# First weight columns ahead of the second chunk of x, three more dummy matmuls, and new stage settings in a gated attention and mixer kernel

## The chip, the cores and the metric

The kernel runs on one core of a Trainium2 chip. The time is device microseconds of one execution, as the median of several; the kernel before took 788.51 us (787.51 to 789.9) in its first three runs; each batch of runs had a chip of its own, and before ran beside it.

Names: PE is TensorE, ACT ScalarE, DVE VectorE, POOL GpSimd, SP the engine that issues most DMA. In the profile, L909 is line 909 of the kernel.

## The reference

```python
def reference(A_x, A_wqkv, A_wo, B_x, B_w1, B_w2, B_w3, B_w4, gate_w):
    def _A_ref(x, wqkv, wo):                     # 32 heads of 16, S = 2048, D = 512
        ...
        scores = jnp.einsum("bhqd,bhkd->bhqk", q, k) * (Dh ** -0.5)
        p = _softmax(scores, axis=-1)
        o = jnp.einsum("bhqk,bhkd->bhqd", p, v)
        return (...)(o, 0, 2, 1, 3).reshape(B, S, D) @ wo
    def _B_ref(x, w1, w2, w3, w4):
        h = _gelu(_layernorm(x, axis=-1) @ w1)
        ...                                      # shifts of h along S by quarters of D
        x1 = x + hs                              # hs = shifted h @ w2
        return x1 + _gelu(_layernorm(x1, axis=-1) @ w3) @ w4
    g = _sigmoid((x * gate_w).sum(-1, keepdims=True))
    return g * a + (1 - g) * b                   # a = _A_ref(x), b = _B_ref(x)
```

There are 32 x 2048 x 2048 exponentials, cut into 2048 score tiles of 128 x 512 with four heads side by side; they are the bulk of the work of ACT and DVE.

## The kernel before

The order of the instructions of every engine is fixed when the kernel is built, by a small model of the engines in Python. The model is steered by some twenty settings, and STAGES overrides them for each stretch of 32 score tiles. Other lines only say what must come before what.

The head: transfers that start before the model does, each with an assumed latency in ns, and dummy matmuls that keep PE busy until x lands.

```python
    xa, xb = (start(e, 3000.0, lambda q, a=a: q.dma_start(out=x_sb[:, a:a + 2, :], in_=x_src(0, a, a + 2)))
              for e, a in (("SP", 0), ("ACT", 2)))
    j_x0 = [xa, xb]
    dl_w["k0"] = start("ACT", 2300.0, col(W("k"), D, D + 128))
    dl_w["q0"] = start("ACT", 2300.0, col(wq, 0, 128))
    j_x1 = [start("SP", 4900.0, lambda q: q.dma_start(out=x_sb[:, 4:8, :], in_=x_src(1, 0, 4)))]
    ...
    def warm_pe():
        for _ in range(8):
            nc.tensor.matmul(sim_ring[RING - 1][:, 0:384], lhsT=zero[:, 0:P], rhs=zero[:], start=True, stop=True)
```

The exponentials on DVE: a pair of tiles is made with a bit trick (L935), and three shifted copies of it follow, on DVE (L971) or on POOL (L974). Which engine makes which copy is up to the settings (GP2, GP3, URG). The model knows that POOL's instructions and these copies exclude each other (`port`).

```python
        for k in range(1, 4):
            def sh(k=k):
                d = [b.slot for b in bufs]
                if alone or k == 1 or k == 2 and not both:
                    nc.vector.tensor_scalar(out=d[k][:, 0:w], in0=d[0][:, 0:w], scalar1=float(SHIFT * k), scalar2=None,
                                            op0=ALU.add)
                else:
                    nc.gpsimd.tensor_scalar(out=d[k][:, 0:w], in0=d[0 if both else 2][:, 0:w], scalar1=1.0,
                                            scalar2=float(SHIFT * (k if both else 1)), op0=ALU.mult, op1=ALU.add)
            ...
                j = dve(0.26 * w + 72.0, pr["jobs"], sh, prio=K.S_PRIO, acq=[bufs[k]], frees=[bufs[0]], port=True)
```

The layer norm (L682): DVE writes a normalised row tile into one of two buffers `xn`, from which a DMA writes it to DRAM, to be read back transposed. The third tile has to wait until the first write is through.

```python
        for t in range(4 * c, 4 * c + 4):
            xb = Buf("xn", 1)
            g = dve(323, [m], lambda t=t, xb=xb: nc.vector.tensor_scalar(
                out=xb.slot[:], in0=x_sb[:, t, :], scalar1=rs[which][:, t:t + 1], scalar2=nm[which][:, t:t + 1],
                op0=ALU.mult, op1=ALU.add), prio=0.35, acq=[xb], port=True)
            ds.append(dma(2200.0, [g], lambda t=t, xb=xb: nc.sync.dma_start(
                out=xn_dram[which, t * P:(t + 1) * P, :], in_=xb.slot[:]), frees=[xb]))
```

The softmax here doesn't subtract the row's maximum and nothing guards it: scores larger than these inputs give would overflow.

## Time and profile before

| before | us |
|---|---|
| profiled span | 787.5 |
| head, up to ACT's first exp | 14.50 |
| body, first to last exp of ACT | 763.20 |
| tail | 9.80 |
| busy in the body: PE, ACT, DVE, POOL | 750.8, 738.0, 737.2, 335.3 |

The cut at ACT's first and last exp parts what can be reasoned about by hand (the head: a chain of transfers and a few instructions) from what cannot (the body: three engines busy for 97 to 98% of it, which hand work to each other). The prediction shows the lines.

### The profile page before, as it was taken

How to read it: one execution, taken by the hardware profiler on the slowest of the kernel's cores; microseconds unless marked ns; L12 is line 12 of the kernel's file. 1: busy time of each engine (PE TensorE's matmuls, PEld its weight loads, DVE VectorE, ACT ScalarE, POOL GpSimd, SP SyncE). 2: the span in 40 equal slices, each digit the busy share in tenths (PEclk: the TensorE clock that was granted, in tenths of full speed). 3: DMA queues.
4: the chain of work that ended last, by engine and by line, in shares of the span. 5: the costliest groups of instructions: out<-in, count | busy, mean ns of one | idle time of the engine just before them, and what ended most of it. 6: DMA issues, size and time to landing. Idle time of an engine off the chain costs nothing.

```text
span 787.5 us, 23893 instructions
## 1 busy us (share of the span) xinstructions
PE 766.7 (97%) x9672; PEld 227.1 (29%) x9672; DVE 744.9 (95%) x1587; ACT 743.3 (94%) x764; POOL 339.2 (43%) x331
## 2 busy tenths in 40 slices
PE   7999999999999999999999999999999999999997
PEld 3433322222222222223222223222223222223222
DVE  4999999999999999999998999899999999999996
ACT  4899999999999999999999999999999999999995
POOL 2234544344546443444244443344434345445352
PEclk9999999999999999999999999999999999999999
DMA  8302113423000320062101001001100000000101
GB/s 204 123 16 46 37 46 80 91 45 113 20 6 20 83 59 20 25 152 62 29 11 32 23 20 46 19 18 36 43 18 20 15 22 26 26 20 20 17 6 44
DMA packets 67093, 34.60 MB, mean 44 GB/s; under 512 B 46748, under 2 KB 62380, under 8 KB 66984
## 3 DMA queue, kind: packets, MB, share of 16 engines
q1 hardware_dynamic: 65512, 32.43, 16.7%
q8 instruction: 75, 1.23, 0.7%
q10 hardware_dynamic: 1472, 0.66, 0.3%
q14 instruction: 34, 0.28, 0.1%
HBM read 17.40 MB, written 6.81 MB: 31 GB/s over the span
## 4 chain that ended last, share of the span: by engine, by line
PE 57%; DVE 23%; ACT 12%; issue 3%; DMA 3%; SPq 1%; POOL 0%; ACTq 0%; POOLq 0%; DVEq 0%
PE acc L1005 20%; PE ring L519 18%; PE psA L829 18%; DVE PD L935 9%; ACT PA L909 9%; DVE PD L971 7%; DMA xn_dram<-xn 1%; PE ring L829 1%; DVE st L662 1%; DMA wq<-in_A_wqkv_dram 1%; DVE V L605 1%; ACT hT L722 1%; ACT hT L753 1%; ACT hB L753 1%; DVE hB L752 1%
## 5 line engine op out<-in xcount | busy, mean ns | idle before, releaser
L909 ACT ACTIVATE PA<-psA 128x1024 bf16<-128x1024 f32 x739 | 693.4, 1040 | 25.0 <-PE acc L1005 8.7
L974 POOL TENSOR_SCALAR PD<-PD 128x1024 uint16<-128x1024 uint16 x269 | 283.8, 1058 | 418.2 <-DVE PD L971 263.0
L935 DVE TENSOR_SCALAR PD<-ring 128x512 uint16<-128x512 f32 x570 | 374.4, 682 | 17.8 <-PE ring L829 15.0
L1005 PE MATMUL acc<-PD,V 128*17 128x512 bf16 x2280 | 302.3, 381 | 2.6 <-DVE accsb L1021 1.4
L829 PE MATMUL psA<-q,kT 32*128 32x512 bf16 x1478 | 284.7, 384 | 3.4 <-ACT PA L909 3.1
L1005 PE MATMUL acc<-PA,V 128*17 128x512 bf16 x1478 | 269.7, 381 | 0.2 <-DVE accsb L1021 0.2
L971 DVE TENSOR_SCALAR PD<-PD 128x1024 uint16<-128x1024 uint16 x586 | 241.4, 453 | 3.5 <-PE acc L1005 1.7
L829 PE MATMUL ring<-q,kT 32*128 32x512 bf16 x570 | 195.4, 384 | 2.8 <-DVE PD L935 2.5
L829 PEld LDWEIGHTS <-kT 32*128 32x128 bf16 x2048 | 73.9, 91 | 306.2 <-issue 305.1
L1005 PEld LDWEIGHTS <-V 128*17 128x17 bf16 x3758 | 74.4, 88 | 141.3 <-issue 119.7
L519 PE MATMUL ring<-xnT,w 128*32 128x512 bf16 x1152 | 91.4, 383 | 1.9 <-DVE qf L588 1.5
L519 PE MATMUL ring<-w,hT 128*32 128x512 bf16 x704 | 58.2, 383 | 0.2 <-DVE PD L935 0.2
L519 PEld LDWEIGHTS <-w 128*32 128x32 bf16 x1920 | 43.5, 95 | 49.7 <-issue 37.8
L1038 POOL TENSOR_TENSOR oT<-accsb,bcs 128x512 bf16<-128x512 f32 x31 | 40.3, 1301 | 10.9 <-DMA bcs<-rr 7.5
L519 PE MATMUL ring<-w,w 128*32 128x256 bf16 (+1 forms) x768 | 41.0, 316 | 0.8 <-DVE PD L935 0.8
L519 PE MATMUL ring<-w,hB 128*32 128x512 bf16 x448 | 35.1, 383 | 0.0
L519 PE MATMUL ring<-w,wq 128*32 128x512 bf16 x256 | 21.2, 398 | 2.8 <-DMA wq<-in_A_wqkv_dram 2.3
L1021 DVE COPY accsb<-acc 128x512 f32<-128x512 f32 x31 | 21.1, 682 | 1.5 <-POOL oT L1038 0.9
L662 DVE BATCH_NORM_STATS2 st<-x_sb 128x6 f32<-128x512 bf16 x32 | 21.6, 682 | 0.0
L519 PEld LDWEIGHTS <-hT 128*32 128x32 bf16 x704 | 14.7, 95 | 19.3 <-issue 14.7
L752 DVE CAST hB<-ring 128x512 bf16<-128x512 f32 x28 | 18.9, 680 | 0.8 <-PE ring L519 0.7
L752 DVE CAST hT<-ring 128x512 bf16<-128x512 f32 x28 | 19.0, 684 | 0.2 <-PE ring L519 0.2
(93 smaller groups left out, 285.2 us busy)
## 6 DMA issues: line engine op xcount, KB each, us to landing
bcs<-rr SPq DMA_DIRECT2D x124, 64.0 KB
xn_dram<-xn SPq DMA_DIRECT2D x32, 128.0 KB
w<-in_B_w_dram SPq DMA_DIRECT2D x5, 512.0 KB
oD<-oT SPq DMA_DIRECT2D x124, 16.0 KB
w<-in_B_w_dram SPq DMA_DIRECT2D x4, 448.0 KB
out_dram<-ot SPq DMA_DIRECT2D x14, 128.0 KB
x_sb<-in_A_x_dram SPq DMA_DIRECT2D x3, 512.0 KB
w<-in_A_wqkv_dram SPq DMA_DIRECT2D x2, 256.0 KB
```

The costliest lines, as they stand in the source:

```text
L519: units.append([Op("col", j, lambda j=j, lf=lf, rf=rf, n0=n0, n1=n1, st=st, sp=sp: nc.tensor.matmul(get()[32 * j:32 * j + 32, n0:n1], lhsT ...
L662: a = dve(600, deps, lambda: nc.vector.bn_stats(out=sb.slot[:], in_=x_sb[:, t, :]), prio=6, at=at, acq=[sb])
L752: pre.append(evac(g, PSUM_NS, lambda ps, m=m: nc.vector.tensor_copy(out=h2()[:, m, :], in_=ps[:])))
L753: ge = act(93 + 427 * FT + 2600, pre, lambda: nc.scalar.activation(out=h2(), in_=h2(), func=ACT.Gelu_apprx_tanh), prio=0)
L829: o = Op("row", i, lambda: nc.tensor.matmul(dst(), lhsT=kT[G][32 * i:32 * i + 32, kt * P:(kt + 1) * P], rhs=qbuf[G, c].slot[32 * i:32 * i ...
L909: job = act(hold, ops, lambda: nc.scalar.activation(out=pb.slot[:, 0:n], in_=buf.slot[:, 0:n], func=ACT.Exp, scale=0.25), acq=[pb], frees= ...
L935: nc.vector.tensor_scalar(out=pr["buf"].slot[:, h * 512:(h + 1) * 512], in0=buf.slot[:], scalar1=BITS_MUL, scalar2=BITS_ADD, op0=ALU.mult, ...
L971: nc.vector.tensor_scalar(out=d[k][:, 0:w], in0=d[0][:, 0:w], scalar1=float(SHIFT * k), scalar2=None, op0=ALU.add)
L974: nc.gpsimd.tensor_scalar(out=d[k][:, 0:w], in0=d[0 if both else 2][:, 0:w], scalar1=1.0, scalar2=float(SHIFT * (k if both else 1)), op0=A ...
L1005: o = Op("col", i, lambda: nc.tensor.matmul(acc[32 * i:32 * i + DH + 1, :], lhsT=lhs(), rhs=rhs(), start=st, stop=True, tile_position=(0, ...
L1021: e = dve(PSUM_NS, round_ops[r], lambda: nc.vector.tensor_copy(out=ab.slot[:], in_=acc[:]), acq=[ab], prio=0)
L1038: n = gp(1250, d3, lambda: nc.gpsimd.tensor_tensor(out=ob.slot[:], in0=ab.slot[:], in1=bb.slot[:], op=ALU.mult), acq=[ob], frees=[ab, bb], ...
```

## The change

Its intent: the first query columns, which the first projection waits for, no longer share the DMA engines with the second chunk of x; more dummies keep PE's clock awake until the projections; and the settings are chosen anew for the changed head.

```diff
-    STAGES = {0: {'DUE_SH': -20, 'AHEAD': 7, 'GP2': 0.35}, 2: {'S_PRIO': 0.324}, ... (cut)
+    STAGES = {0: {'S_PRIO': 0.539, 'DUE_SH': -40}, 1: {'PA_LOW': 1}, 2: {'DVE_WAIT': 2, 'PV_FULL': 0.877}, ... (cut)
@@
-    dl_w["k0"] = start("ACT", 2300.0, col(W("k"), D, D + 128))
-    dl_w["q0"] = start("ACT", 2300.0, col(wq, 0, 128))
+    dl_w["q0"] = start("SP", 2600.0, col(wq, 0, 128))
+    dl_w["k0"] = start("ACT", 2900.0, col(W("k"), D, D + 128))
     j_x1 = [start("SP", 4900.0, lambda q: q.dma_start(out=x_sb[:, 4:8, :], in_=x_src(1, 0, 4)))]
@@
     def warm_pe():
-        for _ in range(8):
+        for _ in range(11):
```

More of the change, by code (lines that the diff above doesn't have):

```diff
@@ L309 @@
     SEG = 32
-    STAGES = {0: {'DUE_SH': -20, 'AHEAD': 7, 'GP2': 0.35}, 2: {'S_PRIO': 0.324}, 3: {'SL': (125, 60), 'AT_SH': 120}, 4: {'ROT': 2, 'DVE_STOP': 7, 'DUE_SH': -8, 'GP2': 0.35}, 5: {'ROT': 2}, 6: {'AHEAD': 8, 'GP2': 0.1, 'P1_PRIO': 0.54}, 7: {'DVE_STOP': 9, 'P1_PRIO': 0.53}, 8: {'DUE_SH': 40, 'URG_L': 19, 'AT_SH': 60}, 9: {'GP2': 0.35, 'DVE_WAIT': 2, 'EARLY': 20, 'PV_IDLE': 0.245}, 10: {'GP3': 0.6}, 11: {'IDLE_NS': 706, 'GP2': 0.35}, 13: {'PV_IDLE': 0.414, 'SL': (5, 60), 'IDLE_NS': 296}, 14: {'GP3': 0.9, 'AT_SH': 120}, 15: {'ROT': 3, 'P1_PRIO': 0.554, 'PV_FULL': 0.948}, 16: {'GP2': 0.1, 'EARLY': 141}, 17: {'AT_SH': 10}, 18: {'GP2': 0.35, 'MAXU': 4}, 19: {'GP2': 0.35, 'P1_PRIO': 0.522, 'SL': (165, 180), 'DVE_WAIT': 2}, 20: {'EARLY': 145, 'S_PRIO': 0.286, 'GP2': 0.1}, 21: {'EARLY': 145, 'S_PRIO': 0.286, 'GP2': 0.1}, 22: {'AHEAD': 11, 'AT_SH': 10, 'EARLY': 51}, 23: {'AT_SH': 10}, 24: {'ROT': 2, 'URG': 3, 'GP3': 0.8}, 25: {'PD_LOW': 2}, 26: {'SL': (125, 60), 'DUE_SH': 40, 'S_PRIO': 0.248, 'AHEAD2': 8}, 27: {'ROT': 1, 'URG_L': 15, 'AHEAD': 12}, 28: {'PRESS': 21, 'P1_PRIO': 0.544, 'S_PRIO': 0.282}, 29: {'PV_IDLE': 0.462, 'DVE_STOP': 4}, 30: {'GP3': 0.9, 'PRESS': 21}, 31: {'GP3': 0.6}, 32: {'DVE_WAIT': 6, 'ROT': 2, 'DUE_SH': 40}, 34: {'DUE_SH': 40, 'DVE_ALONE': 2, 'GP3': 0.6}, 35: {'IDLE_NS': 471, 'DUE_SH': 20, 'DVE_STOP': 5, 'MAXU': 3}, 36: {'GP2': 0.1, 'PRESS': 14}, 37: {'DVE_ALONE': 2, 'DVE_STOP': 3, 'EARLY': 31, 'PA_LOW': 3}, 38: {'PD_LOW': 3, 'EARLY': 55, 'PA_LOW': 2, 'URG': 7}, 39: {'S_PRIO': 0.456, 'AHEAD2': 7, 'EARLY': 155, 'ROT': 1}, 40: {'PA_LOW': 3, 'DVE_ALONE': 2, 'GP3': 0.8}, 41: {'URG': 8, 'URG_L': 19}, 42: {'URG_L': 19, 'PRESS': 39, 'ROT': 1}, 43: {'GP3': 0.8}, 44: {'PD_LOW': 1}, 45: {'DVE_WAIT': 2, 'AHEAD2': 10}, 46: {'GP3': 0.6}, 47: {'DUE_SH': -40, 'EARLY': 79, 'MAXU': 9, 'PA_LOW': 2}, 48: {'DVE_ALONE': 300, 'ROT': 1}, 49: {'AT_SH': 120, 'P1_PRIO': 0.475}, 50: {'IDLE_NS': 896, 'PD_LOW': 2, 'ROT': 2, 'PA_LOW': 1}, 51: {'PD_LOW': 1, 'URG': 6, 'DVE_ALONE': 150, 'IDLE_NS': 830}, 52: {'PRESS': 53, 'EARLY': 6, 'IDLE_NS': 668, 'PV_FULL': 0.848}, 53: {'AHEAD': 12, 'AT_SH': 10, 'PA_LOW': 2, 'ROT': 3}, 54: {'DVE_STOP_L': 6, 'GP3': 0.9}, 55: {'DUE_SH': -40, 'PV_IDLE': 0.253, 'DVE_STOP_L': 10, 'PA_LOW': 2}, 56: {'SL': (25, 60), 'PA_LOW': 2}, 57: {'ROT': 1, 'SL': (85, 60)}, 58: {'GP3': 0.8, 'PD_LOW': 3, 'URG_L': 19}, 59: {'GP2': 0.1}, 60: {'DUE_SH': -20, 'GP3': 0.6, 'P1_PRIO': 0.409}, 61: {'GP2': 0.2}, 62: {'DVE_STOP_L': 10, 'MAXU': 6, 'PA_LOW': 2, 'AHEAD2': 11}, 63: {'DVE_STOP_L': 6, 'MAXU': 6, 'ROT': 1}, 64: {'DVE_STOP_L': 6, 'MAXU': 6, 'SL': (165, 180)}}
@@ new lines @@
+    STAGES = {0: {'S_PRIO': 0.539, 'DUE_SH': -40}, 1: {'PA_LOW': 1}, 2: {'DVE_WAIT': 2, 'PV_FULL': 0.877}, 4: {'GP2': 0.35, 'GP3': 0.8}, 7: {'PV_FULL': 0.918, 'S_PRIO': 0.302}, 8: {'AHEAD2': 6, 'PA_LOW': 0, 'PD_LOW': 1, 'AHEAD': 12}, 9: {'ROT': 3}, 10: {'PD_LOW': 3, 'AHEAD': 12}, 11: {'DVE_STOP_L': 11, 'GP2': 0.35}, 12: {'PRESS': 38, 'AT_SH': 120, 'ROT': 2, 'SL': (5, 20)}, 13: {'DVE_STOP_L': 11, 'PD_LOW': 3}, 14: {'PV_IDLE': 0.491, 'ROT': 3}, 15: {'DVE_WAIT': 5, 'ROT': 2}, 16: {'EARLY': 112, 'DVE_ALONE': 500, 'PD_LOW': 0}, 17: {'ROT': 1, 'DVE_ALONE': 300}, 18: {'AHEAD': 11, 'S_PRIO': 0.52}, 19: {'AT_SH': 60}, 21: {'MAXU': 7, 'PA_LOW': 0, 'IDLE_NS': 490, 'PRESS': 15}, 22: {'AHEAD': 10, 'GP2': 0.2, 'DVE_ALONE': 150, 'MAXU': 11}, 23: {'AT_SH': 10, 'PA_LOW': 0}, 24: {'AT_SH': 10, 'IDLE_NS': 358}, 25: {'PV_FULL': 0.882, 'SL': (125, 140)}, 26: {'PV_IDLE': 0.486, 'DVE_STOP_L': 6, 'DVE_WAIT': 5, 'PV_FULL': 0.856}, 27: {'AT_SH': 120}, 28: {'DVE_WAIT': 2, 'PRESS': 23, 'SL': (5, 20), 'PV_FULL': 0.918}, 29: {'DVE_WAIT': 5, 'DVE_STOP': 4, 'GP2': 0.35, 'DVE_STOP_L': 6}, 31: {'EARLY': 150, 'PD_LOW': 3, 'DUE_SH': 8}, 32: {'DVE_STOP_L': 7, 'S_PRIO': 0.449, 'SL': (25, 60), 'GP2': 0.1}, 33: {'AT_SH': 30, 'GP3': 0.9, 'AHEAD2': 7}, 34: {'PA_LOW': 2, 'P1_PRIO': 0.295}, 35: {'DVE_STOP_L': 9, 'ROT': 2}, 37: {'ROT': 3}, 38: {'P1_PRIO': 0.235, 'PRESS': 14}, 39: {'DVE_ALONE': 300, 'GP2': 0.2}, 40: {'GP3': 0.6, 'PV_FULL': 0.994}, 41: {'PRESS': 15}, 42: {'SL': (205, 60), 'PD_LOW': 2}, 43: {'GP3': 0.9, 'GP2': 0.35}, 44: {'P1_PRIO': 0.218, 'DVE_STOP_L': 9, 'GP2': 0.35, 'IDLE_NS': 726}, 45: {'DVE_STOP_L': 7, 'S_PRIO': 0.577}, 46: {'DVE_WAIT': 6, 'ROT': 2}, 47: {'PV_FULL': 0.857, 'AT_SH': 60, 'DVE_STOP': 8}, 48: {'DVE_ALONE': 0, 'AHEAD': 10, 'DUE_SH': 80, 'ROT': 1}, 49: {'IDLE_NS': 285, 'GP3': 0.8, 'DUE_SH': -8, 'PD_LOW': 1}, 50: {'PD_LOW': 3}, 51: {'GP3': 0.6, 'ROT': 3}, 52: {'PV_FULL': 1, 'DVE_STOP_L': 11}, 53: {'S_PRIO': 0.29, 'DVE_STOP': 5}, 54: {'GP3': 0.8, 'PA_LOW': 2, 'IDLE_NS': 527}, 55: {'DVE_STOP_L': 6, 'P1_PRIO': 0.319, 'S_PRIO': 0.229}, 56: {'GP2': 0.35, 'ROT': 1}, 57: {'AHEAD2': 6, 'PA_LOW': 2, 'IDLE_NS': 417, 'S_PRIO': 0.31}, 58: {'GP2': 0.35}, 59: {'GP2': 0.35}, 60: {'P1_PRIO': 0.366, 'MAXU': 5, 'EARLY': 16, 'GP2': 0.2}, 61: {'AHEAD2': 11, 'PV_FULL': 0.984, 'DVE_STOP': 9}, 62: {'PRESS': 45, 'PD_LOW': 2, 'IDLE_NS': 491, 'P1_PRIO': 0.424}, 63: {'PRESS': 45, 'PD_LOW': 2, 'IDLE_NS': 491, 'P1_PRIO': 0.424}}
```

## The prediction

> **What bounds the kernel now.** I read the busy shares first, then the costliest groups, then busy time by stretch (head, body, tail), then the chain and the TensorE timeline of the first 16 us. The shares say that three engines are loaded alike:
>
> ```profile
> PE 766.7 (97%) x9672; PEld 227.1 (29%) x9672; DVE 744.9 (95%) x1587; ACT 743.3 (94%) x764; POOL 339.2 (43%) x331
> PE   7999999999999999999999999999999999999997
> DVE  4999999999999999999998999899999999999996
> ACT  4899999999999999999999999999999999999995
> ```
>
> Only the first slice (20 us) of DVE and ACT is half empty; the rest is 9 nearly everywhere. The groups show why: softmax's exponentials are shared between ACT (a true exp of two score tiles at a time) and DVE (a bit trick on one tile at a time, whose result is copied with shifts by DVE or POOL and fed four times to PE).
>
> ```profile
> L909 ACT ACTIVATE PA<-psA 128x1024 bf16<-128x1024 f32 x739 | 693.4, 1040 | 25.0 <-PE acc L1005 8.7
> L974 POOL TENSOR_SCALAR PD<-PD 128x1024 uint16<-128x1024 uint16 x269 | 283.8, 1058 | 418.2 <-DVE PD L971 263.0
> L935 DVE TENSOR_SCALAR PD<-ring 128x512 uint16<-128x512 f32 x570 | 374.4, 682 | 17.8 <-PE ring L829 15.0
> ...
> L971 DVE TENSOR_SCALAR PD<-PD 128x1024 uint16<-128x1024 uint16 x586 | 241.4, 453 | 3.5 <-PE acc L1005 1.7
> ```
>
> I cut the span where ACT's first exp starts (14.50 us) and where its last ends (777.7 us). Columns: stretch, its length, then busy us (and instructions) of PE, PEld, DVE, ACT, POOL, then clock, DMA share and GB/s.
>
> ```profile
> 0.00:14.50 14.50, 10.30 (x77) 4.98 (x77) 3.65 (x10) 4.10 (x7) 3.87 (x14) 1.00 0.98 226
> 14.50:777.70 763.20, 750.79 (x9524) 219.08 (x9525) 737.20 (x1570) 737.95 (x756) 335.31 (x317) 1.00 0.16 40
> 777.70:787.50 9.80, 5.62 (x81) 3.00 (x70) 4.02 (x8) 1.29 (x3) 0.00 (x0) 1.00 0.16 54
> ```
>
> In the body ACT idles 763.20 - 737.95 = 25.3 us, DVE 26.0 us. PE idles 12.4 us, but its busy time holds 14.5 us of filler matmuls (line L1265), so its slack is some 27 us. Nothing there is a single bound: three engines hand work to each other, each 3.3 to 3.6% idle. The head is different. There DMA is 0.98 busy, and one wait stands alone (the chain of waits, then PE's timeline):
>
> ```profile
> 1.80 7.10 DMA wq<-in_A_wqkv_dram
> 8.90 0.04 issue
> 8.94 3.60 PE ring L519 x16
> ```
>
> ```profile
> 4.61 2.00 PE L539 MATMUL ring<-idb,x_sb 128*128 128x128 bf16 x16 [0.75 <-DMA x_sb<-in_A_x_dram]
> 8.94 1.90 PE L519 MATMUL ring<-w,wq 128*32 128x512 bf16 x16 [2.33 <-DMA wq<-in_A_wqkv_dram]
> 10.62 1.92 PE L519 MATMUL ring<-w,w 128*32 128x512 bf16 x16
> 12.48 1.03 PE L539 MATMUL ring<-idb,x_sb 128*128 128x128 bf16 x8
> ```
>
> PE has transposed the first chunk of x by 6.6 us and then sits 2.33 us until the query weights land at 8.9 us, 7.1 us after they were issued. After that the first projections take 3.54 us (8.94 to 12.48) for 8 groups of four matmuls, 0.44 us a group, where later in the trace a group of four takes 0.22 us (three groups start at 767.19, 767.40, 767.62). So PE is at half speed until about 12.5 us. The row "PEclk" and the granted clock show 1.00 all the same: this slowness has to be read from durations (634 ns a matmul here, 384 ns later).
>
> **What the Trainium skill says.** (1) "TensorE: Matmul & The Clock Gate", section "What's actually happening": PE starts at 1.2 GHz and goes to 2.4 GHz after about 3.4 us of sustained activity, in a free-running window. The trace agrees in size (0.44 against 0.22 us) and roughly in time: matmuls are continuous from 8.94, and the first fast ones come about 4 us later. (2) The same page, "Part 4: PE-mode transpose", says that transposes do not count as busy in the same way. That fits: eight dummies (1.12 to 3.86 us) and 16 transposes (4.61 to 6.61 us) did not wake the clock here; but it does not prove it, since there was a gap of 0.75 us. (3) "DMA: Bandwidth & Descriptors", "Specifications", wants 512 B or more for line rate. A column load of 128 columns has rows of 256 B: between 9 and 10 us, with such rows almost alone, the DMA view shows 228 GB/s, and 384 GB/s between 4.0 and 4.5 us, when the rows of x (1 KB) move. (4) The same page, "Queues, rings and completion order", has the engines alternate between the queues of SP and ACT. In the trace the ACT queue (x, key and query columns) and the SP queue (second chunk of x) do move side by side.
>
> **The change part by part.** The order of the instructions on PE, DVE and ACT through the whole head is the same in both kernels but for the dummies, so I can shift it by hand.
>
> *Weights first.* The query columns move from third on ACT's queue to second on SP's, ahead of the second chunk of x (512 KB). Until then they shared the DMA engines with that chunk. Now only the two column loads, 1024 packets of 256 B, follow the first chunk. ACT's queue got through its first 512 of them at about 6.2 us while sharing (84, 145 and 224 packets in the half microseconds from 4.5); at the 923 packets per us of 9 to 10 us, 1024 packets from about 4.5 us are through near 5.7 to 6.2, and land by my estimate between 6.3 and 7.2 us. The next bound is then the copies of transposed x: ACT's end at 6.86, DVE's second at 7.41 us. The projection of q can start at 6.7 to 7.3 instead of 8.94 and must end after 7.41. With a cold PE the k projection then starts at about 8.4 to 8.9 instead of 10.62: **1.7 to 2.3 us saved**. The second chunk of x and the first v columns land a little later (I estimate 8.5 and 9.4 us); they are needed at about 10 and 12 us, so no new wait.
>
> *Three more dummies.* Dummies start every 0.32 us, so eleven keep PE streaming from 1.12 to 4.64 us, right up to the first transpose (4.61). Cost: at most 0.05 us. Gain: if the clock is up when the projections start, 8 groups cost 0.22 instead of 0.43 us, **1.7 us less**, less what then waits for the last copy at 7.41, so 1.3 to 1.5 us. The unbroken busy time is 3.5 us by dummies alone, 5.5 us with transposes; a free-running window of 3.4 us fits whole into 5.5 us in (5.5 - 3.4) / 3.4 = 60% of the phases and into 3.5 us nearly never. With transposes counting only in part I give it one half.
>
> Sum for the head: 2.0 + half of 1.4 = **2.7 us**. ACT's first exp starts at 14.5 - 2.7 = 11.8 us, and as ACT ran eleven exps without a gap from 14.50 to 24.9, the shift is passed on and not swallowed.
>
> *Stage settings.* These only reorder and re-divide work. Counting instructions of both kernels: exps on ACT 739 to 736; DVE tiles 570 to 576; DVE shifts 586 to 575; POOL shifts 269 to 289; PE's value matmuls 3758 to 3776 (+24 from DVE tiles, -6 from ACT's); fillers 184 to 208; stretches of score matmuls[...] 738 to 739. By rows: ACT -3 x 693.4/739 = -2.8 us. DVE +6 x 374.4/570 - 11 x 241.4/586 = +3.9 - 4.5 = -0.6 us. PE +18 matmuls at 54 ns (four run side by side in 0.216 us) = +1.0 us, and the fillers sit in gaps. POOL +20 x 1.06 = +21 us of an engine that is 57% idle. If idle times stay as they are, ACT's body becomes 760.4 and DVE's 762.6 us; the slower partner decides, so between -0.6 and -2.8 us. I take **-1.5 us**, which trusts the new choice to be no worse for waits than the old one was.
>
> *Tail.* The same instructions in the same order after the last exp: 0.
>
> Sum: 2.7 + 1.5 = 4.2 us, 788.5 - 4.2 = **784.3 us**.
>
> **The rivals.** (a) *The new order waits more.* The settings are chosen in a model of the engines, and the 25 us of idle time on ACT depend on where that model is wrong. For it: three engines over 94% busy, so each lost handover shows. Idle time up by a tenth costs 2.5 us and eats the gain of the settings: about 786.8. (b) *The new settings fill better.* Eleven fewer shifts on DVE, shorter in latency when POOL has room; a tenth less idle gives 782. (c) *The weights are not the limit, or another transfer takes their place.* All of the early DMA shares the same engines at 0.98; if the key columns or stragglers land only at 8 us, the head gains 1 us: 786. Against it: the projection needs exactly the loads that now come first. (d) *The head's gain is swallowed later*, by a chunk of x or weights that is no earlier than before; DMA is busy until past 26 us. Against it: in the page of waits after 9 us no DMA of these loads is named. It would give 787. (e) *The dummies do nothing*: 785.
>
> **Range and chances.** The runs of before differ by 2.4 us. The head's gain is 1 to 3.7 us, the body's change -4 to +2.5. Added as independent, 8 in 10 lie in 781.5 to 787.0. For a change of 2% (15.8 us) either way I see no mechanism: the whole idle time of ACT in the body is 25 us.
>
> **What would show it.** Right: no wait for wq after 8 us, q projection starting by 7.4; ACT's first exp near 12 us (11 if the clock was up, with 384 ns matmuls in the projections); ACT's and DVE's idle in the body near 25 us. Wrong: a projection starting after 8 us (step on weights), 634 ns matmuls still there (dummies), body from first to last exp longer than 763 us (settings).

## The result, and the profile after

The changed kernel took 786.75 us (786.32 to 786.8) against 788.26 us of before in the same rounds: ratio 0.9977 (95%: 0.996 to 0.9994), a gain of 1.5 us where 4.2 were forecast.

The page of the changed kernel, busy shares and the slices of DVE and ACT (the first digit of each, 20 us, has risen from 4 to 5 and from 4 to 7):

```profile
span 784.2 us, 24044 instructions
...
PE 767.1 (98%) x9717; PEld 227.2 (29%) x9717; DVE 752.8 (96%) x1582; ACT 741.9 (95%) x761; POOL 362.8 (46%) x351
...
DVE  5999999999999999989999999999999999999997
ACT  7899999999999999999999999999999999999995
```

Its costliest groups, in the page's form (line, engine, operation, count, busy us, mean ns, idle before):

```profile
L909 ACT ACTIVATE PA<-psA 128x1024 bf16<-128x1024 f32 x736 | 692.0, 1037 | 28.5 <-PE psA L829 9.2
L974 POOL TENSOR_SCALAR PD<-PD 128x1024 uint16<-128x1024 uint16 x289 | 307.7, 1069 | 396.7 <-DVE PD L971 223.4
L935 DVE TENSOR_SCALAR PD<-ring 128x512 uint16<-128x512 f32 x576 | 377.2, 679 | 11.0 <-PE ring L829 9.5
...
L971 DVE TENSOR_SCALAR PD<-PD 128x1024 uint16<-128x1024 uint16 x575 | 246.4, 468 | 2.4 <-PE acc L1005 0.6
```

Head, body and tail (stretch, length, then PE, PEld, DVE, ACT, POOL busy us, clock, DMA share, GB/s):

```profile
0.00:9.75 9.75, 8.27 (x78) 4.73 (x79) 3.46 (x10) 4.07 (x8) 3.87 (x14) 1.00 0.89 216
9.75:775.10 765.35, 753.92 (x9576) 220.55 (x9575) 745.27 (x1565) 736.56 (x753) 358.94 (x337) 1.00 0.17 42
775.10:784.20 9.10, 4.91 (x70) 1.97 (x65) 4.02 (x8) 1.31 (x3) 0.00 (x0) 0.96 0.18 59
```

PE's timeline of the head (start, length, what, and in brackets the wait before it):

```profile
1.12 3.70 PE L497 MATMUL ring<-zero 128*128 128x384 bf16 x11 [1.12 <-DVE zero L486]
4.62 1.37 PE L539 MATMUL ring<-idb,x_sb 128*128 128x128 bf16 x16
6.22 1.12 PE L519 MATMUL ring<-w,wq 128*32 128x512 bf16 x16 [0.23 <-ACT w L548]
7.15 1.05 PE L519 MATMUL ring<-w,w 128*32 128x512 bf16 x16
8.13 0.62 PE L539 MATMUL ring<-idb,x_sb 128*128 128x128 bf16 x8
```

The head has shrunk from 14.50 to 9.75 us, by 4.75 and not by 2.7: PE waits for ACT's copy, no longer for weights, and the projections run at full speed. The body, which should have shrunk by 1.5 us, has grown from 763.20 to 765.35, by 2.15. DVE shows how: its work in the body was to fall by 0.6 us by counting, and has risen from 737.20 to 745.27, by 8.1. There are 11 fewer shift copies (L971), and they take 246.4 us instead of 241.4, since one takes 468 ns and not 453. ACT does less (736.56 against 737.95) and waits more (28.8 against 25.3 us). The tail lost 0.7 us.

### The profile page after: what moved, and what is told of

Its sections match the earlier page's. It is cut to its first block, busy times and chain, and to the rows that moved or that the text cites. A ratio compares the mean times of both kernels' runs of the same rounds, so it can differ in the third digit from the quotient of the medians. Undisturbed runs are those within 1.5% of the kernel's fastest.

```text
span 784.2 us, 24044 instructions
## 1 busy us (share of the span) xinstructions
PE 767.1 (98%) x9717; PEld 227.2 (29%) x9717; DVE 752.8 (96%) x1582; ACT 741.9 (95%) x761; POOL 362.8 (46%) x351
## 4 chain that ended last, share of the span: by engine, by line
PE 50%; DVE 39%; issue 6%; DMA 2%; ACT 2%; POOL 1%; SPq 1%; DVEq 0%; POOLq 0%; ACTq 0%
PE ring L519 17%; DVE PD L935 16%; PE acc L1005 16%; PE psA L829 15%; DVE PD L971 14%; DVE st L662 1%; DMA pk<-den 1%; DVE accsb L1021 1%; PE ring L829 1%; DVE xn L682 1%; DVE hB L752 1%; ACT hT L753 1%; ACT PA L909 1%; DVE hT L752 1%; DVE V L605 1%
## 5 line engine op out<-in xcount | busy, mean ns | idle before, releaser
L974 POOL TENSOR_SCALAR PD<-PD 128x1024 uint16<-128x1024 uint16 x289 | 307.7, 1069 | 396.7 <-DVE PD L971 223.4
L935 DVE TENSOR_SCALAR PD<-ring 128x512 uint16<-128x512 f32 x576 | 377.2, 679 | 11.0 <-PE ring L829 9.5
L1005 PE MATMUL acc<-PD,V 128*17 128x512 bf16 x2304 | 297.0, 381 | 1.2 <-DVE PD L971 0.7
L1005 PE MATMUL acc<-PA,V 128*17 128x512 bf16 x1472 | 264.7, 381 | 0.7 <-DVE accsb L1021 0.7
L971 DVE TENSOR_SCALAR PD<-PD 128x1024 uint16<-128x1024 uint16 x575 | 246.4, 468 | 2.4 <-PE acc L1005 0.6
L519 PE MATMUL ring<-w,hT 128*32 128x512 bf16 x704 | 55.4, 383 | 1.0 <-DVE PD L935 1.0
L1038 POOL TENSOR_TENSOR oT<-accsb,bcs 128x512 bf16<-128x512 f32 x31 | 41.5, 1339 | 3.5 <-DVE PD L971 2.1
L519 PE MATMUL ring<-w,wq 128*32 128x512 bf16 x256 | 19.6, 383 | 1.0 <-DVE PD L935 0.7
L519 PE MATMUL ring<-wo,oD 128*32 128x512 bf16 x224 | 19.4, 383 | 0.0
```

What stands on the lines that cost most here:

```text
L519: units.append([Op("col", j, lambda j=j, lf=lf, rf=rf, n0=n0, n1=n1, st=st, sp=sp: nc.tensor.matmul(get()[32 * j:32 * j + 32, n0:n1], lhsT ...
L935: nc.vector.tensor_scalar(out=pr["buf"].slot[:, h * 512:(h + 1) * 512], in0=buf.slot[:], scalar1=BITS_MUL, scalar2=BITS_ADD, op0=ALU.mult, ...
L1005: o = Op("col", i, lambda: nc.tensor.matmul(acc[32 * i:32 * i + DH + 1, :], lhsT=lhs(), rhs=rhs(), start=st, stop=True, tile_position=(0, ...
L1038: n = gp(1250, d3, lambda: nc.gpsimd.tensor_tensor(out=ob.slot[:], in0=ab.slot[:], in1=bb.slot[:], op=ALU.mult), acq=[ob], frees=[ab, bb], ...
```

## The experiments

Two things had to be told apart: which part of the change costs what, and by which way the body loses. As the order of the instructions is fixed at build time, it could be checked before a run that with the old settings the new head leaves the order of the rest as it was on every engine, and the same for the new settings with the old head. So head and settings can be exchanged at will.

Measured, in the order of the batches. "First exp" is where ACT's first exp starts in the profiled run; "rest" is the median less the first exp, that is, body and tail.

| kernel | head | dummies | settings | median us (range) | ratio to before (95%) | first exp | rest |
|---|---|---|---|---|---|---|---|
| before | old | 8 | old | 788.09 (785.37 to 788.94) | 1 | 14.50 | 773.6 |
| after | weights first | 11 | new | 786.75 (786.32 to 786.8) | 0.9977 (0.996 to 0.9994) | 9.75 | 777.0 |
| head_new_settings_old | weights first | 11 | old | 786.27 (785.55 to 788.0) | 0.998 (0.9967 to 0.9992) | 9.56 | 776.7 |
| head_old_settings_new | old | 8 | new | 788.97 (787.69 to 790.59) | 1.0013 (1.0 to 1.0025) | 13.19 | 775.8 |
| weights_only | weights first | 8 | old | 783.24 (782.54 to 784.73) | 0.9943 (0.9929 to 0.9956) | 9.59 | 773.7 |
| dummies_only | old | 11 | old | 789.36 (787.7 to 790.55) | 1.0016 (1.0004 to 1.0029) | 13.43 | 775.9 |
| new_settings_8_dummies | weights first | 8 | new | 785.06 (783.45 to 785.88) | 0.9965 (0.9949 to 0.9981) | 9.73 | 775.3 |
| weights_9_dummies | weights first | 9 | old | 783.62 (781.91 to 784.25) | 0.9946 (0.9931 to 0.996) | 9.25 | 774.4 |
| weights_12_dummies | weights first | 12 | old | 785.46 (784.3 to 786.09) | 0.9969 (0.9954 to 0.9983) | 9.68 | 775.8 |
| weights_8_and_3_short | weights first | 8 + 3 short | old | 786.29 (785.34 to 787.11) | 0.9981 (0.9968 to 0.9995) | 9.40 | 776.9 |
| short_136_old_settings | weights first | 136 short | old | 785.19 (784.29 to 786.07) | 0.9973 (0.9954 to 0.9992) | 11.08 | 774.1 |
| short_139_old_settings | weights first | 139 short | old | 787.3 (784.28 to 788.83) | 0.9996 (0.9975 to 1.0016) | 10.59 | 776.7 |
| short_72_old_settings | weights first | 72 short | old | 787.03 (785.6 to 788.59) | 0.9995 (0.9977 to 1.0014) | 10.45 | 776.6 |
| short_136_new_settings | weights first | 136 short | new | 786.22 (785.53 to 787.44) | 0.9987 (0.9969 to 1.0004) | 10.95 | 775.3 |

The first exp comes from one run of each kernel: among eleven profiles with the weights first and at least eight long dummies it lies between 9.21 and 10.02 us, and the two profiles of the old head with eight dummies differ by 1.3 us (14.50 and 13.19; the next section but one says why). So a rest is good to some 0.4 us with the weights first, and to about 1 us with the old head. The batches also ran on different chips: in the batch of the four last kernels before took 786.9 us, 1.2 less than in the row above, so those four compare best among themselves. Where a conclusion below rests on rows of different batches, the ratios to before are given too. Four more kernels, with other buffers or other work on POOL, follow further down.

### Head and settings exchanged

head_new_settings_old is the changed kernel with the old STAGES, head_old_settings_new the kernel before with the new STAGES.

```diff
 # head_new_settings_old, against the changed kernel
-    STAGES = {0: {'S_PRIO': 0.539, 'DUE_SH': -40}, 1: {'PA_LOW': 1}, ... (the new ones)
+    STAGES = {0: {'DUE_SH': -20, 'AHEAD': 7, 'GP2': 0.35}, 2: {'S_PRIO': 0.324}, ... (the old ones)
```

> The changed head (weights first, eleven dummies) with the stage settings of before; the order of all instructions after the head is that of before. Theory S, the new settings cost time: the head is worth all of the 4.75 us by which ACT's first exp came earlier (9.75 against 14.50 us), the body from first to last exp stays at 763 us as before, so about 783.7 us, ratio to before 0.994. Rival L, the body swallows part of an earlier head whatever the settings (a later transfer or handover is no earlier): about 786.7 us, ratio 0.998, with a body of some 766 us.

> The head of before with the new stage settings; the order after the head is that of the changed kernel. Theory S: body some 2 to 3 us longer than before, so about 791 us, ratio 1.003 to 1.004, with DVE busy some 8 us more in the body than before. Rival L: the settings alone are neutral or a gain, 787 to 788.3 us, ratio 0.998 to 1.000.

The new head with old settings gained 1.8 us, though the first exp came 4.9 us sooner. So most of the loss is in the head's own change, not in the settings, which was not expected. The settings alone cost 0.9 us (its interval reaches down to nothing), between what the two theories expected.

### The two parts of the head alone

```diff
 # weights_only, against head_new_settings_old      # dummies_only, against before
-        for _ in range(11):                          -        for _ in range(8):
+        for _ in range(8):                           +        for _ in range(11):
```

> Before, with only the query columns moved ahead of the second chunk of x (eight dummies, old settings). If the weights are the larger half: projection of q starts at 6.7 to 7.3 us, still with 634 ns matmuls, ACT's first exp near 12.2 us and the time near 786 us (ratio 0.997). If the clock comes up here too (transposes count as activity), 384 ns and the first exp near 10.5 us. If another transfer takes the place of the one moved, the start stays after 8 us.

> Before, with only eleven dummies for eight (old DMA order, old settings). If the dummies wake the clock and it outlasts the wait for the query columns (some 2.9 us without matmuls): q projection still at 8.94 us but 384 ns matmuls, first exp near 12.6 us, time near 786.4 us (ratio 0.998). If the clock falls back in that gap: 634 ns, first exp at 14.5 us, ratio 1.000.

weights_only gained 4.9 us, as much as the two profiles' first exps differ by (4.9 us). The dummies alone lost 1.3 us. PE's timeline of weights_only:

```profile
1.12 2.74 PE L497 MATMUL ring<-zero 128*128 128x384 bf16 x8 [1.12 <-DVE zero L486]
4.10 1.73 PE L539 MATMUL ring<-idb,x_sb 128*128 128x128 bf16 x16 [0.24 <-DMA x_sb<-in_A_x_dram]
6.00 1.17 PE L519 MATMUL ring<-w,wq 128*32 128x512 bf16 x16 [0.18 <-ACT w L548]
```

and of dummies_only:

```profile
8.44 1.32 PE L519 MATMUL ring<-w,wq 128*32 128x512 bf16 x16 [2.26 <-DMA wq<-in_A_wqkv_dram]
9.53 1.94 PE L519 MATMUL ring<-w,w 128*32 128x512 bf16 x16
```

Eight dummies are enough once the weights come first: the projections have only 0.18 us of pause before them and run at 379 ns a matmul (median, against 634 before). Within the transposes of weights_only one matmul goes from 314 to 219 ns, at 5.3 us, so PE woke there. With eleven dummies and the weights late, it woke as well, waited 2.26 us, and was slow again for the second projection (1.94 us for 16 matmuls, where the first projection of weights_only needs 1.17). The clock was lost in the wait, and the wait was the weights'. So the gain that the prediction gave to the dummies belongs to the weights, and with them in place the dummies add nothing to the head: first exp at 9.56 us with eleven, 9.59 with eight.

The traces have their own record of the clock, the column before the last two in the view by stretch. It reads 1.00 also where nothing was recorded, and in before the first record comes only at 13.37 us, so the 1.00 in that head is not a reading. Where there are records they agree with the durations, as in dummies_only:

```profile
5.67:9.07 3.40, 1.14 (x21) 0.67 (x22) 0.75 (x2) 1.07 (x2) 0.00 (x0) 1.00 1.32 243
9.08:12.48 3.40, 3.40 (x36) 1.58 (x29) 1.41 (x2) 0.60 (x2) 0.00 (x0) 0.50 1.00 286
```

The clock was full from 5.66 us, half from 9.08 and full again from 12.49. In all traces these stretches are multiples of 3.41 us (but for the last one), and where the windows of 3.41 us lie differs from run to run. head_old_settings_new, whose head is that of before, woke at 4.29 us, before its first transpose (4.42), so eight dummies alone can do it (2.74 us of work in the window); it lost the clock at 7.70 us in the wait for weights, and its first exp came at 13.19 us. before's own profile was not awake until 13.37. The eleven profiles with the weights first woke at 3.8 to 6.3 us and kept the clock. So what moving the weights takes away is the wait in which the clock is lost, and the old head is worth 13.2 to 14.5 us by the position of the window: that the gain in the head (3.6 to 4.9 us) and the gain in time (4.9 us) are equal in the table is partly luck.

### What three dummies cost in the body

The rest says it: with old settings it is 773.7 us with eight dummies and 776.7 with eleven, with the same order of instructions. new_settings_8_dummies asks the same with new settings, the next two vary the number, and the fourth makes the three extra dummies short (16 columns instead of 384).

```diff
 # new_settings_8_dummies, against the changed kernel; weights_9_dummies and weights_12_dummies likewise, old settings
-        for _ in range(11):
+        for _ in range(8):
 # weights_8_and_3_short, against weights_only
-        for _ in range(8):
-            nc.tensor.matmul(sim_ring[RING - 1][:, 0:384], lhsT=zero[:, 0:P], rhs=zero[:], start=True, stop=True)
+        for n in [384] * 8 + [16] * 3:
+            nc.tensor.matmul(sim_ring[RING - 1][:, 0:n], lhsT=zero[:, 0:P], rhs=zero[:, 0:n], start=True, stop=True)
```

> The changed kernel with eight dummies for eleven; weights first and the new settings stay. Theory D, the three dummies cost some 3 us in the body (as between the runs with the old settings, 786.3 and 783.2 us): about 783.8 us, ratio to before 0.994, and the new settings are then neutral. Rival S, the new settings themselves cost 2 to 3 us and the dummies little: about 786.5 us, ratio 0.998. Rival C, chance: small shifts of any kind move the same order by 1 to 2 us either way: anything from 784 to 788.

> Old settings, weights first, nine dummies. Theory D as a cost per dummy (1 us each): 784.2 us, ratio 0.9955. Rival C (scatter by small shifts): anything between 783 and 787 us, not in order of the number of dummies. Rival K (clock): the same as eight if the projections are warm, 783.2 us.

> Old settings, weights first, twelve dummies, which end some 0.3 us after x has landed. Theory D as a cost per dummy: 787.3 us, ratio 0.999. Rival C: anything between 783 and 787 us. If neither: 783.6 us, the head 0.3 us later than with eight.

> Old settings, weights first, eight dummies of 384 columns and three of 16 columns: the number of TensorE instructions is that of eleven, the time that of eight. If the cost goes with the number of instructions before the body (where the instruction stream is fetched in blocks, say): like eleven, 786.3 us, ratio 0.998. If it goes with the time PE is kept busy or with its clock: like eight, 783.2 us, ratio 0.994. Rival C: neither in particular.

Three short dummies, which take PE 0.07 us in all, cost the same 3 us in the body as three long ones. So it is not their time, but that they are there. With the new settings they cost 1.7 us by the medians (785.06 to 786.75), but 0.9 us by the ratios to before (0.9965 to 0.9977, with intervals that overlap), as the two batches ran on different chips.

Where the two traces with old settings part shows one way in which instructions that are over by 5 us can matter at 260 us. A matmul is two instructions (a load of weights and a matmul), 19,344 in the kernel before, and the trace has 75 packets of 16,384 bytes on a queue of kind "instruction" (q8): about one per 256 instructions of PE, one each 10 us. Each keeps one of the 16 DMA engines for 0.9 to 1.6 us. The Trainium skill's page "Runtime: NRT & Kernel Launch", section "Instruction fetch mechanics", says the same: the sequencer fetches 16 KiB blocks of 256 instructions through its own DMA queue, mostly hidden. Six more PE instructions in front move every later block boundary by six instructions. The fetches do follow this count: counted in thirteen of the traces (8 to 139 dummies, from the fourth fetch on), a fetch starts when PE has begun instruction 184 to 190 of a block of 256 in the median, and half of the fetches lie within some 10 instructions of that. The DMA view of 259.5 to 261.1 us (queue: packets, MB, share of 16 engines), weights_only:

```profile
q1 hardware_dynamic: 187, 0.19, 45.2%
```

and head_new_settings_old:

```profile
q1 hardware_dynamic: 174, 0.18, 42.6%
q8 instruction: 1, 0.02, 5.7%
```

In the second, the fetch (259.65 to 261.11 us) falls into two writes of xn. Of their 256 packets 248 are through at 260.34 us, and the last eight, which need the engine that the fetch holds, come after 261.10. In weights_only all 256 are through at 260.29 us, and the fetch starts at 261.14. What follows, on SP (its queue) and on DVE, weights_only:

```profile
261.62 1.47 SPq L692 DMA_TRANSPOSE xnT<-xn_dram  x1
```

```profile
261.63 0.40 DVE L682 TENSOR_SCALAR xn<-x_sb,rs,nm 128x512 bf16<-128x512 bf16 x1
```

and head_new_settings_old:

```profile
262.43 1.18 SPq L692 DMA_TRANSPOSE xnT<-xn_dram  x1
```

```profile
262.38 0.74 DVE L682 TENSOR_SCALAR xn<-x_sb,rs,nm 128x512 bf16<-128x512 bf16 x1 [0.63 <-DMA xn_dram<-xn]
```

DVE needs a free xn buffer and waits 0.63 us. In the waits of DVE between 15 and 770 us (total us, number of waits, longest) this adds up as follows. weights_only:

```profile
DVE xn L682 <- DMA xn_dram<-xn: 1.2, 1, 1.2
DVE pk L1028 <- DMA pk<-den: 0.7, 1, 0.7
```

head_new_settings_old:

```profile
DVE xn L682 <- DMA xn_dram<-xn: 2.9, 3, 1.2
DVE pk L1028 <- DMA pk<-den: 1.8, 2, 1.1
```

With 8, 9, 12, 11 dummies and 8 + 3 short ones the sum of both waits in the profiled run is 1.9, 2.7, 3.5, 4.7 and 5.3 us, and the medians are 783.24, 783.62, 785.46, 786.27 and 786.29: the same order. Where time is lost can be followed exp by exp on ACT: between 219 and 335 us, head_new_settings_old falls behind weights_only by 2.3 us, the kernel with 8 + 3 by 2.7, that with 12 by 1.8 and that with 9 by 0.1.

### More buffers for xn

If part of the cost goes by way of the two xn buffers, four of them should take that part away. Buffers of their own do not fit (209.84 kB a partition asked for, 207.87 there), so the space of hB and hT, which is free at those times, was lent. The order of the instructions is unchanged.

```diff
 # four_xn_8_dummies, against weights_only; four_xn_11_dummies likewise with 11
+            i = t % 4
+            xa_ = lambda ...: (hB[:, i * 512:(i + 1) * 512] if which == 0 or c < 2
+                               else hT[:, i, 512:1024] if c == 2 else xb.slot[:])
-                out=xb.slot[:], in0=x_sb[:, t, :], ...
+                out=xa_(), in0=x_sb[:, t, :], ...
-                out=xn_dram[which, t * P:(t + 1) * P, :], in_=xb.slot[:]), frees=[xb]))
+                out=xn_dram[which, t * P:(t + 1) * P, :], in_=xa_()), frees=[xb]))
```

> Weights first, old settings, eight dummies, same order; but the normalised rows of x get four buffers instead of two (borrowed from the gelu tiles while these are idle), so that DVE no longer waits for the write of xn to land before it fills a buffer again. Theory F (blocks of TensorE's instruction stream, 16 KB each, hold up small transfers, and DVE waits for these in its fixed order): the 1.2 us of such waits in this build go, about 782.1 us, ratio to before 0.993. If the waits are only a symptom: unchanged, 783.2 us.

> The same with eleven dummies. Theory F: the 2.9 us of waits for xn seen in the build with eleven dummies go; what is left of the difference to eight is the wait for pk (1.9 against 0.7 us): about 783.5 us, ratio 0.994. If the eleven cost 3 us by another way: still about 786 us, 3 to 4 us above the run with eight.

| kernel | median us (range) | ratio to before (95%) |
|---|---|---|
| four_xn_8_dummies | 781.98 (780.5 to 782.98) | 0.9922 (0.9908 to 0.9936) |
| four_xn_11_dummies | 783.64 (782.02 to 786.02) | 0.995 (0.9935 to 0.9966) |

With eleven dummies this gives back 2.6 us (786.27 to 783.64), with eight 1.3, and the cost of the three dummies falls from 3.0 to 1.7 us; by the ratios, as the batches ran on different chips, it falls from 2.9 to 2.2. So between a quarter and nearly half of it went by way of xn, with intervals of over 1 us on each figure. The rest is left. In the profile of four_xn_11_dummies all of the 4.0 us of DVE's waits for transfers are for pk, the sums of softmax on their way through DRAM; that profile was of its slowest run (786.02 us). No run took these waits away. four_xn_8_dummies is the fastest kernel with a right result: it beats before by 0.8% and the changed kernel by 0.6%.

### Is it the phase of the blocks, or any added instruction?

So far the phase was read from one place in a trace and from an order of five numbers. It makes a sharp forecast: 128 more matmuls are 256 instructions, one whole block, and should cost the body nothing, while three more on top should cost 3 us again.

```diff
 # short_136_old_settings, against weights_only; also with 139 and 72, and with 136 against the changed kernel
-        for _ in range(8):
-            nc.tensor.matmul(sim_ring[RING - 1][:, 0:384], lhsT=zero[:, 0:P], rhs=zero[:], start=True, stop=True)
+        for _ in range(136):
+            nc.tensor.matmul(sim_ring[RING - 1][:, 0:16], lhsT=zero[:, 0:P], rhs=zero[:, 0:16], start=True, stop=True)
```

> Weights first, old settings; the eight dummies of 384 columns are replaced by 136 of 16 columns. A TensorE matmul is two instructions (a weight load and a matmul), so 128 more are 256 instructions, one whole block of the instruction stream. If the three dummies cost time because they shift which instruction the blocks of 256 begin at, this kernel has the same phase as the one with 8 dummies and should take its time again: ratio 0.994, some 783.2 to 783.8 us (short dummies took some 23 ns each, so 136 end near 4.3 us, where x lands at 4.1: at most 0.3 us later in the head), with under 2.5 us of VectorE waits for transfers of xn and den in the body. If the cost comes from any extra instruction ahead of the body, or from the dummies' effect on the head, it should be at 786 or more, as with 11.

> As the run with 136 short dummies, with three more: the phase of 11 dummies. By the phase theory some 786.3 us, 2.5 to 3 us slower than the run with 136, with 4 us or more of VectorE waits for transfers. By the rival (nothing but the head's work counts, or extra instructions as such), equal to the run with 136 within 0.5 us.

> As above with 72 short dummies: half a block further than 8 (64 matmuls, 128 instructions). The phase theory says only that the time is another draw, between 782 and 787, and that it goes with the VectorE waits for transfers in its profile (below 3 us of waits: under 784; above 4 us: over 785.5). The head is as early as with 8 or up to 0.3 us later if the clock of TensorE does not wake.

> The changed kernel with 136 short dummies in place of 11: the phase of 8 dummies. Phase theory: the time of the new settings with 8 dummies, 785.1 us (ratio 0.9965), 1.5 us below the changed kernel. Rival: 786.7 or more.

The total times missed what was expected, since the head was worse than thought: the short dummies did not wake PE, and the first exp came at 11.08 us instead of 9.59. PE's timeline of short_136_old_settings:

```profile
1.12 3.79 PE L497 MATMUL ring<-zero 128*128 128x16 bf16 x136 [1.12 <-DVE zero L486]
4.77 1.87 PE L539 MATMUL ring<-idb,x_sb 128*128 128x128 bf16 x16
6.57 2.06 PE L519 MATMUL ring<-w,wq 128*32 128x512 bf16 x16
8.38 1.15 PE L519 MATMUL ring<-w,w 128*32 128x512 bf16 x16
```

PE was busy without a pause from 1.12 us and still slow until 8.4. In the body the forecast held with the old settings. The rest with 136 is 774.1 us, near the 773.7 with eight and not near 776.7; with 139 it is 776.7, that of eleven. In the batch itself 136 beat 139 by 2.1 us in the median, although its first exp came 0.5 us later; five of the six runs of 139 are slower than every run of 136, and one is not (784.28). That one was profiled: its body is as short as that of 136, and its waits of DVE are 3.4 us where 4 or more were expected. With the new settings the rest is 775.3 us with 136 dummies and with eight, 777.0 with eleven; but three chips are behind these figures, and taken by the ratios to before the rest with 136 lies midway between the two, so that pair decides nothing. So with the old settings it is mainly the phase of the blocks that costs, and not the number of instructions; a second batch with 8, 11, 136 and 139 side by side was not run.

Another expectation fell: 72 dummies, half a block away, should have followed the waits of DVE in the profile. These were 2.1 us, and the median was 787.03. The profiled run was its fastest (785.6), and even so it does not fit. DVE's waits for xn and pk are thus not the whole way from the phase to the time. The profile of 72 shows another one. PE idled 0.5 us twice shortly before 297.7 us, and then had half its clock for one window of 3.4 us:

```profile
297.77:301.17 3.40, 3.40 (x29) 0.76 (x28) 3.14 (x7) 1.89 (x2) 1.04 (x1) 0.50 0.05 10
```

Matmuls took up to 634 ns there, and exp by exp the kernel fell 1.5 us behind weights_only. It was the only profile with such a window in the body, and the other five runs of 72 had a mean clock of 0.999 or 1.000, so this does not explain their times.

### What the new settings cost

At the phase of eight dummies the settings cost some 1.7 us (1.2 to 2.2; rests of 773.6, 773.7 and 774.1 with the old, 775.8, 775.3 and 775.3 with the new). By counting they should save. The suspect is the copies L971, which got longer. In the trace of before 132 of the 586 overlap an instruction of POOL, and take 569 ns in the mean; the others take 419. After, 168 of 575 do, and take 597 ns, the others 415. These means hide two kinds: most copies that overlap take their usual time (a median of 419 to 421 ns), and 24 before and 37 after take over 600 ns, up to 1.5 us. Beside POOL's own copies (L974) alone there are 14 such before and 26 after. One of them in the timeline of the changed kernel, where the second of two copies starts 0.08 us after a copy on POOL, ends 0.27 us after it, and takes 1.27 us:

```profile
73.75 1.60 DVE L971 TENSOR_SCALAR PD<-PD 128x1024 uint16<-128x1024 uint16 x2
74.00 1.08 POOL L974 TENSOR_SCALAR PD<-PD 128x1024 uint16<-128x1024 uint16 x1 [0.94 <-DVE PD L971]
```

The Trainium skill's page "SBUF — State Buffer", section "Who interferes with whom", has the reason: DVE in its fast two-port mode, which such a copy can enter, and POOL take turns at one pair of ports, and whoever comes second waits for the whole instruction of the other. The times of these long copies fit. To test that this eats the gain, POOL's copies were cut to 32 of 1024 columns, with a wrong result (the first use of each buffer is at full width, so that nothing unwritten is read).

```diff
 # narrow_pool_old_settings, against weights_only; narrow_pool_new_settings, against new_settings_8_dummies
-                    nc.gpsimd.tensor_scalar(out=d[k][:, 0:w], in0=d[0 if both else 2][:, 0:w], scalar1=1.0,
+                    v = w if id(d[k]) not in seen else 32; seen.add(id(d[k]))
+                    nc.gpsimd.tensor_scalar(out=d[k][:, 0:v], in0=d[0 if both else 2][:, 0:v], scalar1=1.0,
```

> Weights first, eight dummies, old settings, same order, but the shift copies on GpSimd cover 32 columns instead of 1024 (a wrong result on purpose). Theory P (GpSimd and VectorE hinder each other): no shift copy of DVE over 600 ns, DVE busy in the body down by some 18 us of excess, time down by 2 to 6 us as PE and ACT become the only bounds. If DVE's long copies cost nothing: 783.2 us unchanged.

> The same with the new settings (eight dummies; 785.1 us with full width; wrong on purpose). Theory P: the excess of 30 us of DVE time goes as well, and the new settings are no longer slower than the old ones: within 1 us of the narrow run of the old settings or faster by up to 2 us. If the new settings lose by their order and not by the longer DVE copies: still 1.5 to 2 us slower than the narrow run of the old settings.

| POOL's copies | old settings | new settings | new less old |
|---|---|---|---|
| full (8 dummies) | 783.24 | 785.06 | +1.8 |
| 32 columns (8 dummies) | 771.37 (ratio 0.9792) | 769.42 (ratio 0.9767) | -2.0 |

The group L971 at full width, weights_only and new_settings_8_dummies:

```profile
L971 DVE TENSOR_SCALAR PD<-PD 128x1024 uint16<-128x1024 uint16 x586 | 238.7, 447 | 3.5 <-PE acc L1005 1.7
```

```profile
L971 DVE TENSOR_SCALAR PD<-PD 128x1024 uint16<-128x1024 uint16 x575 | 245.3, 466 | 2.4 <-PE acc L1005 0.6
```

and with narrow copies on POOL, old and new settings:

```profile
L971 DVE TENSOR_SCALAR PD<-PD 128x1024 uint16<-128x1024 uint16 x586 | 225.8, 426 | 3.5 <-PE acc L1005 1.7
```

```profile
L971 DVE TENSOR_SCALAR PD<-PD 128x1024 uint16<-128x1024 uint16 x575 | 222.1, 427 | 2.5 <-PE acc L1005 0.7
```

Without POOL beside them, 11 fewer copies do save DVE 3.7 us (225.8 to 222.1) and the program 2.0, near the 1.5 that the prediction gave to the settings. With POOL beside them they cost DVE 6.6 us more (238.7 to 245.3) and the program 1.8. Two expectations missed: 9 and 10 copies over 600 ns were left (nearly all beside L1038, another instruction of POOL), and the times fell by 11.9 and 15.6 us, where 2 to 6 were expected for the old settings. With the old settings the gain is nearly the whole 12.9 us by which DVE's copies became shorter in sum, so other gains are probably in it. The caveat: narrow copies also finish sooner, so PE's value matmuls are free earlier; the test shows that POOL's long copies turn the gain into a loss, and the durations that DVE is blocked beside them, but not how much of the loss goes that way. The full-width figures also come from two batches; within one batch, the new settings cost 0.9 us (old head) and 1.0 us (136 short dummies).

## Why the prediction was right or wrong

The ledger of shown steps, from the medians: 788.1 - 4.9 (weights first, to 783.24) + 1.8 (settings, to 785.06) + 1.7 (three dummies, to 786.75) = 786.7. These medians are from three batches; by the ratios to before the steps are -4.5, +1.7 and +0.9 us. The time lies in the predicted range, but two of the three terms had the wrong sign, and the third was forecast at less than half of what it is.

*Weights first*: right in kind, mis-sized at 2.0; it is 4.9 us. No wait for wq is left, and the projection starts at 6.00 to 6.22 us, sooner than the 6.7 to 7.3 that I took for the bound by copies. One reading behind my landing times was low: the 228 GB/s of 256 B rows is the mean of a stretch whose last fifth is nearly idle, and before that it is 268. The other half is the interaction that I did not see: the wait for the late weights was also where PE lost a clock that eight dummies can raise. I costed the projections cold with eight dummies, while without the pause PE was awake for them in every profile. That the gain is passed on to the end and not swallowed was right within what the old head varies by: 3.6 to 4.9 us of head, 4.9 us of time.

*Three more dummies*: the step that failed. I gave them half of 1.4 us, with a cost of "at most 0.05 us", by looking only at the place where they run. The half chance of waking PE rested on a window of 3.4 us that is busy throughout; head_old_settings_new woke on 2.74 us of dummies in 3.41, so eight were enough for that. Their gain in the head is nil once the weights come first, and their cost is 0.9 to 1.7 us with the new settings and 3.0 with the old, all of it in the body. That it is the three instructions and not their time is shown (three short ones cost the same); that it goes by the phase of PE's instruction blocks is supported by 136 against 139, and the way from there to the time is known only in part. Rival (e), "the dummies do nothing", was nearer, and still missed the sign.

*Stage settings*: the second step that failed, -1.5 predicted, +1.8 measured with eight dummies. (With eleven it is +0.5, 786.27 to 786.75, as the phase costs the old order more.) In my sum for DVE the term for tiles held (+3.9 predicted, 377.2 - 374.4 = +2.8 measured), and the term for copies was mis-sized: 11 copies less by their old mean is -4.5 us, and measured was +5.0. The mean of a group is no constant when the change shifts 20 copies to POOL: more of those left run beside POOL, and more of them are long (37 over 600 ns, where it was 24). I had costed POOL's 21 us as "an engine that is 57% idle", and left out what POOL takes from DVE while it is busy. Rival (a), "the new order waits more", foresaw 786.8 for the kernel, and the sum is right, but its reason is only partly so: ACT idles 3.5 us more in the body, while DVE idles 6 us less and is busy 8 us more.

*Tail*: 0 predicted, -0.7 in the profile, which is within what runs differ by.

What stays open: why some phases are good and others bad beyond the one place shown; by which way the part of the dummies' cost goes that four xn buffers leave, and nearly all of that with 72; and why single runs of one kernel differ by 2 to 4.5 us.

## What to carry to other kernels

Before paying for a warm clock, take away the wait that lets it go cold, and look at more than one profile: whether the same head woke PE differed between two runs here. Cost an instruction moved to POOL not only by POOL's idle time, but by the DVE copies that it will block. In a kernel tuned to a fixed order, as this one is, a few instructions added ahead can move the time by a few tenths of a per cent through the phase of instruction fetches, so an edit of this size is judged only against versions with the same number of instructions ahead (or a whole 256 more), and buffers that a DMA frees late are worth doubling first.

## What the Trainium skill lacked or had wrong

- "Runtime: NRT & Kernel Launch" has the 256-instruction blocks and calls their cost mostly hidden. It lacks that a fetch holds up other engines' small transfers: 0.9 to 1.7 us of one DMA engine per block here, and six PE instructions ahead of the body moved the time by 3.0 us with the old settings, while 256 more left the body within 0.4 us by the medians, 0.9 by the ratios.
- "TensorE: Matmul & The Clock Gate" says that transposes do not count as busy in the same way. Here they count for something. With 139 short dummies, transposes from 4.85 us and projections from 6.65, the clock was full from 7.50 us: the window of 3.41 us before it held only 0.85 us of projections. In before, a window with 1.0 us of projections and hardly anything else (6.54 to 9.95 us, counted back from 13.37) did not wake PE. And the short dummies are not the reason, which the page lacks: in short_136_new_settings a window full of matmuls of 16 columns (1.49 to 4.90 us, counted back from 8.31) did not wake PE, while eight of 384 columns did in head_old_settings_new (4.29 us).
- No page has that the view's granted clock reads 1.00 where the trace has no record yet, as in the head of before, where matmuls took 634 instead of 379 ns. Where there are records it shows the gate: 0.50 in dummies_only from 9.08 us.
- "SBUF — State Buffer" has the port pair that DVE and POOL take turns at, and the runs agree. It gives no measure of how often it bites: 168 of 575 copies at 597 instead of 415 ns after, 132 of 586 at 569 before; of these, 37 and 24 took over 600 ns.
